# A three-stage kernel on one core: the last layer's products on the two row halves of TensorE

## The chip, the cores and the metric

The kernel runs on one core of one Trainium2 chip. The metric is the device time of one execution in microseconds (us), as the median of several runs. Engines are named as in the profile: PE is TensorE's matmul, PEld its weight load, DVE VectorE, ACT ScalarE, POOL GpSimd, SP the engine that issues most DMAs.

## What is computed

Causal attention for 2 batches of 12 heads, sequence 448, head size 64; its output, 896 rows of 768, goes through two blocks of two matrix products each:

```
attn_out = softmax(mask(q @ k.T / 8)) @ v            # (2, 12, 448, 64)
x = attn_out.transpose(0, 2, 1, 3).reshape(896, 768)
h = x @ w_in;  g = max(h, 0) + alpha * min(h, 0)      # 768 -> 2048, layer 1
x = g @ w_out                                         # 2048 -> 768, layer 2
h = x @ w_in2; g = h if h >= 1, 0 if h <= -1, else (h + 1)^2 / 4   # layer 3
out = g @ w_out2                                      # 2048 -> 768, layer 4
```

The weights of the two blocks are eight-byte floats; all else is f32.

## The kernel before, in words

Attention comes first and is pipelined over 12 head pairs; in it, `scores` (line 448) multiplies the two heads of a pair on the two row halves of TensorE, 64 rows each, into two banks of PSUM, and for the last tile of a head pair line 441 multiplies all 128 rows. Both are plain f32.

Then `run_layer` runs the four layers one after another. Activations lie transposed in SBUF: 128 rows of a feature tile by 448 tokens of a batch b (0 or 1), as a pair of planes in the type fp32r, the rounded value and the rest (`x_t`, `g_t`). A weight is split into two such parts by `Weights`: a chunk is loaded on SP (`load`, L109), its high words pass ACT (`magnitude`, L122), DVE rebuilds f32 values from integer halves in four steps (L141 to L160), ACT rounds (L169) and DVE takes the rest (L173). Three buffers hold split chunks, two the raw words.

Layers 2 and 4 have 6 output tiles m of 128 features, and for each 4 chunks of 4 feature tiles: 16 steps k. `products` issues for each k three products per batch: high weight with both planes, low weight with the high plane. Each is one matmul of 128 rows, 128 columns of weights and 448 moving columns, with its own weight load; that is 6 x 16 x 6 = 576 matmuls in layer 4. Layers 1 and 3 have as many with 16 tiles f of 6 steps.

PSUM has 8 banks here: three buffers of two banks (`pair`, pool ps_s) and two of one bank (`single`, pools ps_3 and ps_o). A tile m takes one pair, a bank for each batch; the last tile of layer 4 takes the two single banks, and its last chunk does all products of b = 0 before those of b = 1.

The order of instructions on each engine is the order of the code (`manual_schedule`). After the products of a chunk, `interleave` issues the split steps of a later chunk in turn with what is `late`: the moving out of the tile before. For layer 4 that is `evac_out`: ACT copies the first 224 columns and SP stores them, DVE copies the other 224 and ACT's queue stores them. The last tile has `evac_first` for b = 0 and `evac_last` for b = 1, which copies 320 and 128 columns on DVE.

Of the kernel before, what the change touches and what calls it, by code (L numbers as in the profile page):

```python
# [8 lines left out]
F32 = mybir.dt.float32  # L9
# [13 lines left out]
def attention_moe_moe_kernel(ctx: ExitStack, tc: tile.TileContext, qk, v, w1, w2, w3, w4, alpha, out):  # L23
# [8 lines left out]
    nc = tc.nc  # L32
    NP, _, _, S = qk.shape
    NB = 2
# [251 lines left out]

        return [high, low]

    def evac_out(ps, m, b):
        o = ep.tile([128, S], F32, tag="act_g", name="o_sb")  # L290

        def store():
            for i, (copy, queue) in enumerate(((nc.scalar.copy, nc.sync), (nc.vector.tensor_copy, nc.scalar))):
                c = slice(i * S // 2, (i + 1) * S // 2)
                copy(o[:, c], ps[:, c])  # L295
                queue.dma_start(out=out[m * 128:(m + 1) * 128, b * S + c.start:b * S + c.stop], in_=o[:, c])

        return [store]

    def evac_first(ps, m, b):  # L300
        for op in evac_out(ps, m, b):
            op()

    def evac_last(ps, m, b):
        o = ep.tile([128, S], F32, tag="act_g", name="o_sb")
        for c, queue in ((slice(0, 320), nc.sync), (slice(320, S), nc.scalar)):
            nc.vector.tensor_copy(o[:, c], ps[:, c])
            queue.dma_start(out=out[m * 128:(m + 1) * 128, b * S + c.start:b * S + c.stop], in_=o[:, c])

    def interleave(a, b):  # L310
        a, b = list(a), list(b)
        while a or b:
            for ops in (a, b):
                if ops:
                    ops.pop(0)()

    def pair():
        return ps_s.tile([128, 2, 512], F32, tag="s", name="ps")

    def single(pool):  # L320
        return pool.tile([128, 512], F32, tag="s", name="ps1")

    def products(ps, ws, src, k, kk, first, last):

        for part in range(2):
            for b in ps:
                for xp in range(2 - part):
                    nc.tensor.matmul(  # L328
                        ps[b][:, :S],
                        lhsT=ws[:, part, k * 128:(k + 1) * 128],  # L330
                        rhs=src[b, kk][:, xp],
                        start=first and part == 0 and xp == 0,
                        stop=last and part == 1,
                    )

    def early_tile():

        ws = wts.next()
        ps = {b: single((ps_3, ps_o)[b]) for b in range(NB)}
        early[0] = ws, ps  # L340
        for part in FILL:
            for b, ks in part:
                for k in ks:
                    products({b: ps[b]}, ws, x_t, k, k, k == 0, False)
            yield

    def run_layer(layer, late):

        if layer in (1, 3):
            mt, nch, kc, src = NF, 1, KD, x_t  # L350
        else:
            mt, nch, kc, src = NM, NC2, KC, g_t
        evac = {1: act_prelu, 2: evac_x, 3: act_quad, 4: evac_out}[layer]
        for m in range(mt):
            ps = {}
            for ch in range(nch):
                if layer == 1 and m in early:
                    ws, ps = early.pop(m)
                    products(ps, ws, src, kc - 1, kc - 1, False, True)
                else:  # L360
                    ws = wts.next()
                if ch == 0 and layer == 4 and m == mt - 1:
                    rest = {b: single((ps_3, ps_o)[b]) for b in range(NB)}
                elif ch == 0:
                    t = None if ps else pair()
                    rest = {} if ps else {b: t[:, b] for b in range(NB)}
                else:
                    rest = ps

                end = layer == 4 and m == mt - 1 and ch == nch - 1  # L370
                for group in [{b: p} for b, p in rest.items()] if end else [rest] if rest else []:
                    for k in range(kc):
                        kk = ch * kc + k
                        products(group, ws, src, k, kk, kk == 0, kk == nch * kc - 1)
                    if end:
                        for b, p in group.items():
                            (evac_last if b == NB - 1 else evac_first)(p, m, b)
                ps = {**ps, **rest}
                if wts.n_used > 1 and not early:
                    interleave(wts.split_ops(), late)  # L380
                    late = []
                    wts.run(wts.load())
                    wts.run(wts.magnitude())
            late = [] if end else [op for pair in zip(*(evac(ps[b], m, b) for b in range(NB))) for op in pair]
        return late


    class Attention:
# [143 lines left out]
        def evac(self, p):  # L532
            b, m = divmod(p, NP // NB)
            return evac_x(self.o.pop(p), m, b)

    with tc.manual_schedule():
# [4 lines left out]
        def step(gen, n):  # L541
# [4 lines left out]
        ps_s, ps_3, ps_o = (  # L546
            ctx.enter_context(tc.tile_pool(name=f"ps_{n}", bufs=b, space=PSUM))
            for n, b in (("s", 3), ("3", 1), ("o", 1))
        )
        with ExitStack() as pa:  # L550
# [12 lines left out]
            at.clear_v()  # L563
            early = {}
            fill = early_tile()
            steps = wts.prime()
            prime = []
# [96 lines left out]
        ep = ctx.enter_context(tc.tile_pool(name="ep", bufs=2))  # L664
        late = []
        for layer in (1, 2, 3, 4):
            late = run_layer(layer, late)
            if layer % 2 == 0:
                interleave(late, [])
                late = []  # L670
# [44 lines left out]
```

## Time and profile before

| | us |
|---|---|
| runs | 545.83, 547.82, 545.70 |
| median | 545.83 |
| span of the profiled execution | 544.2 |
| TensorE matmul busy in it | 538.2 |
| weight load, DVE, ACT, POOL busy | 476.0, 416.4, 240.9, 138.5 |
| layer 4, first to last matmul's start | 423.4 to 539.9 |

The span goes from the first to the last instruction of one profiled execution, whose time beside the span is not given; the median of the runs is 1.6 us above it. The groups of the page's part 5 count instructions of one line with their mean duration. A matmul's duration overlaps its neighbours', so the pace of a stream is the distance of starts.

### The profile page before, as it was taken

What the parts mean: (1) busy time and instruction counts of PE and PEld (TensorE: products, weight loads), DVE (VectorE), ACT (ScalarE), POOL (GpSimd) and SP (SyncE); (2) the same over time, 40 slices, a digit from 0 to 9 for tenths busy, and PEclk for the clock granted to TensorE, in tenths of its full rate; (3) what the DMA queues carried; (4) which work ended last, traced back from release to release, by engine and by line L of the source; (5) the groups of instructions that cost most, each with busy time, mean ns of one, the idle gap of its engine ahead of it and who ended that gap; (6) DMA issues with size and microseconds to landing.
All of it is one profiled execution on the core that took longest, in us unless ns stands there. A gap on an engine that the chain in (4) does not pass through costs nothing.

```text
span 544.2 us, 8503 instructions
## 1 busy us (share of the span) xinstructions
PE 538.2 (99%) x3055; PEld 476.0 (87%) x3055; DVE 416.4 (77%) x790; ACT 240.9 (44%) x504; POOL 138.5 (25%) x190
## 2 busy tenths in 40 slices
PE   8999999999999999999999999999999999999997
PEld 4666689999999999999999999999999999999996
DVE  5899879888889987576566699888898865755740
ACT  7999953333333333232323255555555332322310
POOL 5777822333333420000000023333333200000000
PEclk9999999999999999999999999999999999999999
DMA  6555313333332234342344333333322243434421
GB/s 186 185 157 171 91 59 117 116 117 116 117 93 80 88 91 134 97 142 92 94 139 120 114 119 113 117 116 117 115 70 70 95 144 123 151 111 133 136 71 34
DMA packets 25339, 61.90 MB, mean 114 GB/s; under 512 B 3537, under 2 KB 13009, under 8 KB 25297
## 3 DMA queue, kind: packets, MB, share of 16 engines
q1 hardware_dynamic: 22992, 59.58, 34.8%
q10 hardware_dynamic: 2304, 1.79, 1.0%
q8 instruction: 24, 0.39, 0.3%
q14 instruction: 19, 0.15, 0.1%
HBM read 58.60 MB, written 2.75 MB: 113 GB/s over the span
## 4 chain that ended last, share of the span: by engine, by line
PE 93%; ACT 3%; DVE 1%; POOL 1%; issue 0%; DVEq 0%; POOLq 0%
PE ps L328 86%; PE ps L527 3%; ACT pexp L468 2%; PE ps L448 2%; PE ps L510 1%; PE ps L441 1%; POOL pexp L485 1%; PE ps L71 1%; DVE pexp L459 1%; DVE pt L616 0%; ACT pt L634 0%; ACT pt L632 0%; ACT x L282 0%; ACT w_split L169 0%; ACT pt L633 0%
## 5 line engine op out<-in xcount | busy, mean ns | idle before, releaser
L328 PE MATMUL ps<-x,w_split 128*128 128x448 f32 x1152 | 234.2, 365 | 0.0
L328 PE MATMUL ps<-g,w_split 128*128 128x448 f32 x1152 | 233.8, 365 | 0.0
L328 PEld LDWEIGHTS ps<-g,w_split 128*128 128x128 f32 x1152 | 216.4, 188 | 17.1
L328 PEld LDWEIGHTS ps<-x,w_split 128*128 128x128 f32 x1152 | 216.2, 188 | 17.1
L246 POOL TENSOR_TENSOR g<-act_g,g 128x448 fp32r<-128x448 f32 x64 | 85.6, 1338 | 265.7 <-ACT g L245 265.6
L169 ACT CAST w_split<-w_f 128x512 fp32r<-128x512 f32 (+2 forms) x81 | 56.8, 701 | 126.8 <-DVE w_f L160 87.0
L173 DVE TENSOR_TENSOR w_split<-w_f,w_split 128x512 fp32r<-128x512 f32 (+1 forms) x78 | 64.1, 822 | 50.2 <-ACT w_split L169 50.0
L245 ACT CAST g<-act_g 128x448 fp32r<-128x448 f32 x64 | 36.2, 565 | 76.5 <-DVE act_g L258 66.5
L141 DVE TENSOR_SCALAR w_f<-w_f 128x512 f32<-128x512 f32 (+2 forms) x81 | 58.5, 722 | 8.3 <-ACT w_f L122 8.2
L154 DVE SCALAR_TENSOR_TENSOR w_f<-w_raw,w_f 128x512 uint32<-128x512 uint32 (+2 forms) x81 | 63.7, 786 | 1.5
L160 DVE SCALAR_TENSOR_TENSOR w_f<-w_raw,w_f 128x512 uint32<-128x512 uint32 (+2 forms) x81 | 63.6, 786 | 1.4
L122 ACT ACTIVATE w_f<-w_raw 128x512 f32<-128x512 f32 (+2 forms) x84 | 62.0, 739 | 0.1
L468 ACT ACTIVATE pexp<-pexp,stat 128x128 f32<-128x128 f32 (+3 forms) x84 | 43.7, 527 | 2.3 <-DVE stat L459 2.0
L485 POOL TENSOR_SCALAR pexp<-pexp,stat 128x384 f32<-128x384 f32 (+3 forms) x79 | 39.9, 527 | 15.0 <-DVE stat L477 13.8
L147 DVE TENSOR_SCALAR w_f<-w_f 128x512 uint32<-128x512 uint32 (+2 forms) x81 | 38.5, 475 | 1.5
L270 ACT ACTIVATE act_t<-act_t,half 128x448 f32<-128x448 f32 x32 | 21.5, 671 | 37.3 <-DVE act_t L269 37.3
L459 DVE CUSTOM_DVE_ANT_0 pexp<-ps,mask 128x128 f32<-128x128 f32 (+3 forms) x84 | 33.4, 447 | 5.0 <-POOL ident masks.py:199 3.5
L285 DVE TENSOR_TENSOR x<-ps,x 128x448 fp32r<-128x448 f32 x24 | 14.8, 618 | 17.5 <-ACT x L282 17.5
L295 DVE COPY o_sb<-ps 128x224 f32<-128x224 f32 x11 | 4.3, 392 | 28.3 <-ACT o_sb L295 28.3
L448 PEld LDWEIGHTS ps<-qk 64*128 64x128 f32 x144 | 12.9, 196 | 12.7 <-DVE pt L629 4.6
L527 PE MATMUL ps<-pt,v 128*64 128x448 f32 (+3 forms) x192 | 23.2, 385 | 0.0
L269 DVE TENSOR_SCALAR act_t<-ps 128x448 f32<-128x448 f32 x32 | 19.8, 620 | 2.8 <-PE ps L328 2.2
(45 smaller groups left out, 236.9 us busy)
## 6 DMA issues: line engine op xcount, KB each, us to landing
w_raw<-w SPq DMA_DIRECT2D x48, 512.0 KB, 3.6
w_raw<-w SPq DMA_DIRECT2D x29, 768.0 KB, 4.3
qk<-qk SPq DMA_DIRECT2D x10, 448.0 KB, 3.8
w_raw<-w SPq DMA_DIRECT2D x9, 256.0 KB, 4.2
out<-o_sb SPq DMA_DIRECT2D x11, 112.0 KB, 1.7
out<-o_sb ACTq DMA_DIRECT2D x11, 112.0 KB, 1.7
v<-v SPq DMA_DIRECT2D x12, 56.0 KB, 3.8
v<-v SPq DMA_DIRECT2D x12, 48.0 KB, 3.3
```

What stands on the lines that cost most here:

```text
L122: nc.scalar.activation(out=f32(w[:, c]), in_=f32(hi[:, c]), func=AF.Abs)
L141: nc.vector.tensor_scalar(out=f32(w[:, c]), in0=f32(w[:, c]), scalar1=HI_MIN, scalar2=HI_MAX, op0=ALU.max, op1=ALU.min)
L154: nc.vector.scalar_tensor_tensor(out=w[:, c], in0=hi[:, c], scalar=0xC0000000, in1=w[:, c], op0=ALU.bitwise_and, op1=ALU.bitwise_or)
L160: nc.vector.scalar_tensor_tensor(out=w[:, c], in0=lo[:, c], scalar=29, in1=w[:, c], op0=ALU.logical_shift_right, op1=ALU.bitwise_or,)
L169: nc.scalar.copy(s[:, 0, c], f32(w[:, c]))
L173: (side or nc.vector).tensor_sub(s[:, 1, c], f32(w[:, c]), f32(s[:, 0, c]))
L246: nc.gpsimd.tensor_sub(t[:, 1, :], g, f32(t[:, 0, :]))
L328: nc.tensor.matmul(ps[b][:, :S], lhsT=ws[:, part, k * 128:(k + 1) * 128], rhs=src[b, kk][:, xp], start=first and part == 0 and xp == 0, st ...
L459: nc.vector.tensor_tensor_reduce(out=self.pexp[p][:, o:o + w], in0=b[:, :w], in1=mask3 if i == 3 else mask[:, 384 - w:], scale=-SCALE, sca ...
L468: nc.scalar.activation(out=e, in_=e, func=AF.Exp, bias=self.st[p][:, 0, n:n + 1], scale=-1.0, accum_out=self.st[p][:, 1, n:n + 1],)
L485: nc.gpsimd.tensor_scalar(out=e, in0=e, scalar1=self.st[p][:, 2, n:n + 1], scalar2=1.0, op0=ALU.mult, op1=ALU.mult)
L527: nc.tensor.matmul(ps[j * D:(j + 1) * D, c * 128:S], lhsT=t[:, c, j, :], rhs=pt[:, 2 * c + j, c * 128:], start=c == 0, stop=c == NQ - 1,)
```

## The change

In layer 4 each product becomes two, on rows 0 to 63 and on rows 64 to 127, each half into a bank of its own; ACT copies the second half's bank to SBUF and DVE adds the first half's bank to it when the tile is moved out. A tile m takes four banks: two pairs for even m, one pair and the two single banks for odd m.

```
-    def evac_out(ps, m, b):
+    def evac_out(ps, m, b, parts=((0, S),)):
         o = ep.tile([128, S], F32, tag="act_g", name="o_sb")
+        t = ep.tile([128, S], F32, tag="act_t", name="o_half")
 
         def store():
-            for i, (copy, queue) in enumerate(((nc.scalar.copy, nc.sync), (nc.vector.tensor_copy, nc.scalar))):
-                c = slice(i * S // 2, (i + 1) * S // 2)
-                copy(o[:, c], ps[:, c])
-                queue.dma_start(out=out[m * 128:(m + 1) * 128, b * S + c.start:b * S + c.stop], in_=o[:, c])
+            for i, (lo, hi) in enumerate(parts):
+                c = slice(lo, hi)
+                nc.scalar.copy(t[:, c], ps[1][:, c])
+                nc.vector.tensor_add(o[:, c], ps[0][:, c], t[:, c])
+                queue = nc.scalar if (i + b) % 2 else nc.sync
+                queue.dma_start(out=out[m * 128:(m + 1) * 128, b * S + lo:b * S + hi], in_=o[:, c])
...
     def evac_last(ps, m, b):
-        o = ep.tile([128, S], F32, tag="act_g", name="o_sb")
-        for c, queue in ((slice(0, 320), nc.sync), (slice(320, S), nc.scalar)):
-            nc.vector.tensor_copy(o[:, c], ps[:, c])
-            queue.dma_start(out=out[m * 128:(m + 1) * 128, b * S + c.start:b * S + c.stop], in_=o[:, c])
+        for op in evac_out(ps, m, b, ((0, 256), (256, S))):
+            op()
...
+    def products_rows(ps, ws, src, k, kk, first, last):
+
+        for part in range(2):
+            for b in ps:
+                for xp in range(2 - part):
+                    for h in range(2):
+                        r = slice(h * 64, h * 64 + 64)
+                        nc.tensor.matmul(
+                            ps[b][h][:, :S],
+                            lhsT=ws[r, part, k * 128:(k + 1) * 128],
+                            rhs=src[b, kk][r, xp],
+                            start=first and part == 0 and xp == 0,
+                            stop=last and part == 1,
+                        )
+
+    def four_banks(m):
+
+        t = [pair(), pair()] if m % 2 == 0 else [pair()]
+        banks = [t_[:, i] for t_ in t for i in range(2)]
+        if m % 2:
+            banks += [single(ps_3), single(ps_o)]
+        return {b: banks[2 * b:2 * b + 2] for b in range(NB)}
...
-                if ch == 0 and layer == 4 and m == mt - 1:
-                    rest = {b: single((ps_3, ps_o)[b]) for b in range(NB)}
+                if ch == 0 and layer == 4:
+                    rest = four_banks(m)
...
-                        products(group, ws, src, k, kk, kk == 0, kk == nch * kc - 1)
+                        (products_rows if layer == 4 else products)(
+                            group, ws, src, k, kk, kk == 0, kk == nch * kc - 1
+                        )
```

On PE, the end of the last chunk (g1_12 to g1_15 are feature tiles of b = 1; a row counts matmuls in a row with the same bank and the same tile) reads before:

```order
L328 MATMUL ps1_5024<-g0_15_4299,w_split_5091 128x448 x3
L328 MATMUL ps1_5025<-g1_12_4125,w_split_5091 128x448 x3
L328 MATMUL ps1_5025<-g1_13_4189,w_split_5091 128x448 x3
L328 MATMUL ps1_5025<-g1_14_4253,w_split_5091 128x448 x3
L328 MATMUL ps1_5025<-g1_15_4305,w_split_5091 128x448 x3
```

and with the change, for the last of these rows:

```order
L344 MATMUL ps1_5514<-g1_15_4330,w_split_5627 128x448
L344 MATMUL ps1_5515<-g1_15_4330,w_split_5627 128x448
L344 MATMUL ps1_5514<-g1_15_4330,w_split_5627 128x448
L344 MATMUL ps1_5515<-g1_15_4330,w_split_5627 128x448
L344 MATMUL ps1_5514<-g1_15_4330,w_split_5627 128x448
L344 MATMUL ps1_5515<-g1_15_4330,w_split_5627 128x448
```

The three matmuls of a step into one bank have become six, in turn into two.

On ACT, from the last weight chunk to the end of the kernel (ps1 are single banks, o_half is the copy of the second half), before:

```order
L122 ACTIVATE w_f32_5065<-w_raw_5018 128x512
L169 CAST w_split_5091<-w_f32_5065 128x512
L295 COPY o_sb_5134<-ps1_5024 128x224
L296 DMA out<-o_sb_5134 128x224
L308 DMA out<-o_sb_5151 128x128
```

and with the change:

```order
L169 CAST w_split_5627<-w_f32_5577 128x512
L296 COPY o_half_5707<-ps_5513 128x448
L296 COPY o_half_5736<-ps1_5515 128x256
L299 DMA out<-o_sb_5735 128x256
L296 COPY o_half_5736<-ps1_5515 128x192
```

ACT has two copies of the last tile where it had none, and the DMA issue of that tile's first part now stands between them.

On DVE, where a tile m is moved out between the split steps of a weight chunk, before:

```order
L141 TENSOR_SCALAR w_f32_4869<-w_f32_4869 128x512
L295 COPY o_sb_4871<-ps_4722 128x224
L147 TENSOR_SCALAR w_f32_4869<-w_f32_4869 128x512
L295 COPY o_sb_4872<-ps_4722 128x224
L154 SCALAR_TENSOR_TENSOR w_f32_4869<-w_raw_4832,w_f32_4869 128x512
```

and with the change:

```order
L141 TENSOR_SCALAR w_f32_5259<-w_f32_5259 128x512
L297 TENSOR_TENSOR o_sb_5261<-ps_5016,o_half_5262 128x448
L147 TENSOR_SCALAR w_f32_5259<-w_f32_5259 128x512
L297 TENSOR_TENSOR o_sb_5263<-ps1_5017,o_half_5264 128x448
L154 SCALAR_TENSOR_TENSOR w_f32_5259<-w_raw_5198,w_f32_5259 128x512
```

The two copies of 224 columns have become two adds of 448, at the same places.

## Rows read from the trace of the kernel before

**Rows 1.** Page, parts 1 and 2: busy us (share), and granted clock in tenths.

```profile
PE 538.2 (99%) x3055; PEld 476.0 (87%) x3055; DVE 416.4 (77%) x790; ACT 240.9 (44%) x504; POOL 138.5 (25%) x190
...
PEclk9999999999999999999999999999999999999999
```

**Rows 2.** Chain of waits from 423.4 us to the end: start, length, what.

```profile
423.34 116.95 PE ps L328 x577
540.29 0.02 issue
540.32 0.49 DVE o_sb L307
540.81 0.20 DVEq L711
```

**Rows 3.** Source view of L328 from 330 us: ns min/median/max, first and last start.

```profile
L328 PEld LDWEIGHTS ps<-g,w_split x576: 187/188/188, 423.2 to 539.7; 128*128 128x128 f32 x192
L328 PE MATMUL ps<-g,w_split x576: 362/365/369, 423.4 to 539.9; 128*128 128x448 f32 x192
```

**Rows 4.** Windows of layer 4: length, busy us of each engine, clock, DMA.

```profile
423.00:443.00 20.00, 20.00 (x100) 18.54 (x99) 14.62 (x24) 7.14 (x12) 2.71 (x2) 1.00 0.32 105
443.00:462.00 19.00, 19.00 (x95) 17.61 (x95) 11.96 (x22) 5.47 (x10) 0.00 (x0) 1.00 0.43 136
...
521.00:541.00 20.00, 19.28 (x96) 17.52 (x94) 7.02 (x14) 2.71 (x6) 0.00 (x0) 1.00 0.11 35
```

**Rows 5.** Timeline, narrow windows near 7 us (start, length, engine, line): f32, all rows.

```profile
7.04 0.54 PE L441 MATMUL ps<-qk,qd 128*128 128x448 f32 x1
7.41 0.54 PE L441 MATMUL ps<-qk,qd 128*128 128x448 f32 x1
7.79 0.54 PE L441 MATMUL ps<-qk,qd 128*128 128x448 f32 x1
```

**Rows 6.** Timeline, narrow windows at 41 us: all rows, then pairs of row halves.

```profile
40.66 0.54 PE L441 MATMUL ps<-qk,qd 128*128 128x448 f32 x1
41.13 0.59 PE L448 MATMUL ps<-qk 64*128 64x384 f32 x2
...
41.56 0.49 PE L448 MATMUL ps<-qk 64*128 64x384 f32 x2
41.88 0.38 PE L448 MATMUL ps<-qk 64*128 64x256 f32 x2
41.88 0.19 PEld L448 LDWEIGHTS ps<-qk 64*128 64x128 f32 x2
42.09 0.38 PE L448 MATMUL ps<-qk 64*128 64x256 f32 x2
42.10 0.19 PEld L448 LDWEIGHTS ps<-qk 64*128 64x128 f32 x2
```

**Rows 7.** Waits from 423 us (total us, times, longest); then groups (busy us, mean ns).

```profile
ACT w_split L169 <- PE ps L328: 10.6, 4, 2.7
...
L328 PE MATMUL ps<-g,w_split 128*128 128x448 f32 x576 | 116.9, 365 | 0.0
L328 PEld LDWEIGHTS ps<-g,w_split 128*128 128x128 f32 x576 | 108.2, 188 | 8.5
```

**Rows 8.** Timeline of DVE at 419 us: the end of f = 14 in layer 3.

```profile
419.42 0.62 DVE L273 TENSOR_TENSOR act_g<-ps,act_t 128x448 f32<-128x448 f32 x1
```

**Rows 9.** Groups by line and shape, 78 us to the end: busy us, mean ns, idle.

```profile
L282 ACT CAST x<-ps 128x448 fp32r<-128x448 f32 x12 | 5.8, 536 | 18.0 <-PE ps L328 18.0
L295 ACT COPY o_sb<-ps 128x224 f32<-128x224 f32 x11 | 3.8, 347 | 31.1 <-PE ps L328 26.7 <-DVE w_f L147 4.4
...
L285 DVE TENSOR_TENSOR x<-ps,x 128x448 fp32r<-128x448 f32 x13 | 8.0, 621 | 16.6 <-ACT x L282 16.6
L295 DVE COPY o_sb<-ps 128x224 f32<-128x224 f32 x11 | 4.3, 392 | 28.3 <-ACT o_sb L295 28.3
L307 DVE COPY o_sb<-ps 128x320 f32<-128x320 f32 x1 | 0.5, 492 | 1.6 <-PE ps L328 1.6
L307 DVE COPY o_sb<-ps 128x128 f32<-128x128 f32 x1 | 0.3, 281 | 0.0
```

**Rows 10.** Timeline of the end: start us, length, engine, line, [idle before].

```profile
537.92 0.35 ACT L295 COPY o_sb<-ps 128x224 f32<-128x224 f32 x1 [9.40 <-PE ps L328]
538.30 0.33 SPq L296 DMA_DIRECT2D out<-o_sb  x1
538.30 0.39 DVE L295 COPY o_sb<-ps 128x224 f32<-128x224 f32 x1 [9.05 <-ACT o_sb L295]
...
539.91 0.37 PE L328 MATMUL ps<-g,w_split 128*128 128x448 f32 x1
540.32 0.69 DVE L307 COPY o_sb<-ps 128x320 f32<-128x320 f32 x2 [1.62 <-PE ps L328]
540.84 0.33 SPq L308 DMA_DIRECT2D out<-o_sb  x1
541.04 0.34 ACTq L308 DMA_DIRECT2D out<-o_sb  x1
```

## The prediction

> **What bounds the kernel now.** I read the profile's first two parts: in [rows 1] the reader sees TensorE busy for 538.2 of 544.2 us, weight loads 476.0, VectorE 416.4, and a granted clock in the top tenth in every slice. Then the chain of waits from 423.4 us on, where the last layer begins [rows 2]: one piece of products, 116.95 us, then only 0.7 us of VectorE and queue. Nothing outside TensorE's matmul stream ends anything in this stage. The source view of L328 [rows 3] gives its pace: 576 matmuls on g, first start 423.4, last 539.9, so 116.5 / 575 = 0.2026 us from start to start. The windows of the stage [rows 4] give a granted clock of 1.00 throughout, which is the 2.4 GHz level. At that level 448 columns, one each cycle, are 448 / 2.4 = 186.7 ns. So each matmul takes **16 ns more** than its columns, and 576 × 16 = 9.2 us of the layer are this excess. What the change can win is inside those 9.2 us; all else it does is on engines with room or at the very end.
>
> **What the trace says of row halves.** Attention has them already: line 448 multiplies 64 rows at a time, each half into its own bank, in plain f32. Compare it with line 441, plain f32 over all 128 rows. In [rows 5] three neighbouring starts of 448-column matmuls are 7.04, 7.41 and 7.79: 0.375 us each, two cycles per column (0.3733) and about 2 ns. In [rows 6] two half matmuls start together (the rows count x2) at 41.56, the next two at 41.88, the next two at 42.09 us: 0.32 us for a pair of 384 columns (two cycles each: 0.320) and 0.21 to 0.22 for a pair of 256 (0.2133). So a **pair of halves takes the time of one full matmul**, not of two and not less. Their two weight loads are together as well: 0.19 us for two, as long as one of all rows lasts (188 ns, [rows 3]). That supports replacing one full product by two half products at no cost, and it shows no gain, because per row half the columns to stream and the columns to load stay the same: 448 and 128.
>
> **The change part by part.**
>
> *Products.* Out go 576 full matmuls, in come 1152 half matmuls, 576 pairs, each with the columns of the one it replaces. The clock stays at its level, since the stream has no gaps. Where is the 16 ns from? The full f32 row shows about 2 ns of it in any matmul; the other 14 belong to this one-cycle-per-column form with a load beneath each, which no row shows in halves. Bounds from rows: the pair runs like the f32 rows, 0.1867 + 0.002 = 0.1887, a gain of 0.0139 × 576 = 8.0 us; or the 14 ns are paid by each half's load in turn, 0.2026 + 0.0139, a loss of 8.0 us. The far end is two halves in turn, 2 × 0.2026. I take **0.2026, change 0.0**: the nearest rows are the full form in this stage and the pairs of line 448, where halving rows changed nothing in time per column. An excess that came from a load reading beside a stream would come in both halves at once, since both load at once.
>
> The Trainium skill, page "TensorE: Matmul & The Clock Gate", section "The mechanism", says a weight load overlaps a matmul in flight only when the row group differs; that speaks for the change. Here 188 ns loads lie under matmuls of the same rows, 108.2 us of loads in 116.9 ([rows 7]), so this trace does not bear it out beyond the 14 ns; by that rule the sum would be the first rival's. The Trainium skill, page "TensorEngine Tiling (Array Packing)", section "Theoretical Speedup", speaks against it: it gives a gain only where a dimension is at most 64, and this contraction has 128; the sum by it would be the one I take.
>
> *Change of mode.* From full rows to halves in attention: 40.66 to 41.13 is 0.47 us where 0.375 is the pace [rows 6], so 0.1 us, once, where layer 4 begins. **+0.1 us.**
>
> *Banks.* An m tile takes four banks instead of two. At the start of the layer the second pair is the one of f = 14 in layer 3, whose last reader ends at 419.42 + 0.62 = 420.04 us [rows 8], 3.3 us before the first product at 423.4. After that even and odd m use different banks, so a bank is reused after a whole tile of about 19.4 us, and its readers need about 2.5. **0.**
>
> *Moving a tile out.* Per (m, b) a 224-column copy on each of ACT and VectorE (347 and 392 ns) becomes a 448-column copy on ACT (like line 282, 536 ns) and an add of 448 on VectorE (like line 285, 621 ns) [rows 9]. Per m tile that is 2 × 229 = 0.46 us more on VectorE and 0.38 on ACT. VectorE is busy 11.96 of 19 us in such a stretch [rows 4]. The low_bits and high_bits steps of the weight chunk stand behind the adds on VectorE, and the hi_part cast behind the store's DMA issue on ACT; who waits for those is a chunk whose cast already waits for TensorE to free its buffer (10.6 us in 4 waits, [rows 7]), so the chunks are ahead. On SP the store of b = 0 now waits for the add, about 0.8 us later, and the next weight load behind it waits for a raw buffer that VectorE frees later still. The cover is that lead; if it were gone, 0.46 us for each of 5 tiles, 2.3 us, would show. **0.**
>
> *The end.* Before: the last matmul starts at 539.91, VectorE copies 320 and 128 columns from 540.32, and the last DMA is issued at 541.04 [rows 10], 0.72 us after the first copy began. Now for b = 1 the order on ACT is copy 256, DMA issue (which waits for the add of 256), copy 192; the add of 192 and its SP issue follow. ACT copies: 347 ns at 224 and 536 at 448 give 0.37 for 256 and 0.32 for 192. Adds: 621 at 448, less 1.1 ns a column (from 0.492 at 320 and 0.281 at 128), 0.41 and 0.34. Issue on ACT 0.34, four hand-overs of about 0.03 (538.27 to 538.30), 0.05 for the sequencer. In all 0.37 + 0.41 + 0.34 + 0.05 + 0.32 + 0.34 + 0.12 = 1.95 against 0.72: **+1.2 us**. If ACT can start its second copy without the issue's 0.34, it is 0.9. The tile of b = 0 is stored under b = 1's last 12 products (2.4 us).
>
> **Sum:** 0 + 0.1 + 0 + 0 + 1.2 = +1.3 us on the profiled span of 544.2, so 545.5. The runs shown have a median of 545.83, 1.6 us above that span; I leave that rest as it is: **547.1 us**, +0.24%. A measurement of this kernel can tell about 0.5% from no change, 2.7 us.
>
> **The rivals.**
>
> *The load's share goes away.* If the 14 ns are the price of a full-array load under a full-array matmul, and a half's load hides under the other half, a pair takes 0.1887: -8.0 + 1.3 = -6.7, **539.1 us**. For it: full f32 matmuls have 2 ns of excess and these 16, so something in the one-cycle form is not hidden. Against it: the halves run in step, so a half's load lies beside its own half's matmul as before. It passes the 0.5% line once 7 ns a pair are won (4.0 us).
>
> *Two loads, two excesses* (the other side). The 14 ns are a stall that each load gives the whole array, and a pair has two loads: 0.2165 a pair, +8.0 + 1.3, **555.1 us**. Place: the weight loads of L344, every pair. It decides from 2.5 ns a pair ((2.7 - 1.3) / 576). For it: the loads double from 576 to 1152. Against it: in line 448 two loads at once cost no more than one.
>
> *No overlap.* The halves of this form take turns, and the change doesn't do what it says: 576 × 0.2026 = +116.7 us, **664 us**. For it: line 448's pairs write each bank at half the pace that these would. Against it: those pairs are in step in every row read.
>
> *The lead is used up* on VectorE or the tail is longer than summed: +2.3 more, **549.4 us**.
>
> **How the numbers follow.** The forecast 0.52 (its own range 546.0 to 548.5), the load's share 0.20, two excesses 0.15, no overlap 0.06, lead used up 0.07. The range runs from the first rival's time to the second's, 539.0 to 555.5, and leaves out turns and what lies beyond. Faster by over 0.5%: 0.20. Within: the forecast and a third of the last, 0.54. Slower: 0.15 + 0.06 + the rest of the last, 0.26.
>
> **What would show it.** In the profile after: 576 pairs of g matmuls from about 423.4, starts of pairs 0.203 apart (0.189: first rival; 0.216: second; 0.405: turns), weight loads x1152, the chain still one piece of products, VectorE waiting for TensorE and not the reverse, and between the last matmul and the last DMA issue 2.3 us instead of 1.1. A wait of TensorE on VectorE or ACT anywhere after 423 us, or a granted clock under 1.00, would make the sum wrong.

## The result and the profile after

The changed kernel takes **548.86 us** (median of 5 runs, 548.55 to 549.68) against 545.70 us; the ratio is 1.0051, 95% interval 1.0033 to 1.0069. It is half a percent slower: the forecast's sign and range held, its size did not (+1.3 us were summed; the ratio gives 2.8, the medians differ by 3.2).

The profiled execution has a span of 547.0 us, 2.8 more than before. The page's parts 1 and 2, first lines:

```profile
span 547.0 us, 9642 instructions
PE 539.7 (99%) x3631; PEld 475.8 (87%) x3631; DVE 418.7 (77%) x790; ACT 243.2 (44%) x506; POOL 138.2 (25%) x190
...
PEclk9999999999999999999999999999999999999999
```

The counts of TensorE grew by 576, VectorE and ScalarE are busy 2.3 us longer each, and the clock stayed where it was in [rows 1]. The chain of waits from the start of layer 4 (start, length, what) answers to [rows 2]:

```profile
423.05 119.24 PE ps L344 x1146
...
542.38 0.38 ACT o_half L296
...
542.78 0.44 DVE o_sb L297
...
543.24 0.34 ACTq L299
...
543.62 0.33 ACT o_half L296
...
543.97 0.36 DVE o_sb L297
```

Still one piece of products, and no wait of TensorE on another engine; the products are 119.24 us instead of 116.95, and behind them stands a chain of five steps. The source view of L344 (ns min/median/max, first and last start) gives the pace, as [rows 3] did:

```profile
L344 PEld LDWEIGHTS ps<-g,w_split x1152: 182/184/186, 423.0 to 541.7; 64*128 64x128 f32 x192
L344 PE MATMUL ps<-g,w_split x1152: 358/365/469, 423.0 to 541.9; 64*128 64x448 f32 x192
```

576 pairs from 423.0 to 541.9: 118.9 / 575 = 0.2068 us a pair, against 0.2026 for a full matmul. The end, to be read beside [rows 10]:

```profile
541.28 1.00 PE L344 MATMUL ps<-g,w_split 64*128 64x448 f32 x6
...
542.38 0.37 ACT L296 COPY o_half<-ps 128x256 f32<-128x256 f32 x1 [1.95 <-PE ps L344]
542.78 0.42 DVE L297 TENSOR_TENSOR o_sb<-ps,o_half 128x256 f32<-128x256 f32 x1 [1.69 <-ACT o_half L296]
543.24 0.34 ACTq L299 DMA_DIRECT2D out<-o_sb  x1
543.62 0.32 ACT L296 COPY o_half<-ps 128x192 f32<-128x192 f32 x1 [0.87 <-DVE o_sb L297]
543.97 0.36 DVE L297 TENSOR_TENSOR o_sb<-ps,o_half 128x192 f32<-128x192 f32 x1 [0.76 <-ACT o_half L296]
544.35 0.33 SPq L299 DMA_DIRECT2D out<-o_sb  x1
```

From the last matmul's start (541.9) to the last DMA issue are 2.44 us, before 1.13; from that issue to the end of the span 2.65, before 3.16. So the 2.8 us of the two spans are: layer 4 began 0.4 earlier (423.0 for 423.4; attention and layers 1 to 3 are unchanged, so this is a difference between two executions), its products took 118.9 - 116.5 = **2.4 us longer**, the way from the last matmul to the end **0.8 us longer**.

### The profile page after: what moved, and what is told of

Its sections match the earlier page's. It is cut to its first block, busy times and chain, and to the rows that moved or that the text cites. A ratio compares the mean times of both kernels' runs of the same rounds, so it can differ in the third digit from the quotient of the medians.

```text
span 547.0 us, 9642 instructions
## 1 busy us (share of the span) xinstructions
PE 539.7 (99%) x3631; PEld 475.8 (87%) x3631; DVE 418.7 (77%) x790; ACT 243.2 (44%) x506; POOL 138.2 (25%) x190
## 4 chain that ended last, share of the span: by engine, by line
PE 92%; ACT 4%; DVE 2%; POOL 1%; DMA 1%; ACTq 0%; issue 0%; POOLq 0%
PE ps L329 64%; PE ps L344 22%; PE ps L553 3%; ACT pexp L494 2%; PE ps L474 2%; PE ps L536 1%; PE ps L467 1%; DMA qk<-qk 1%; POOL pexp L511 1%; DVE pexp L485 1%; DVE pt L642 0%; ACT pt L660 0%; ACT pt L658 0%; ACT x L282 0%; ACTq L445 0%
## 5 line engine op out<-in xcount | busy, mean ns | idle before, releaser
L344 PE MATMUL ps<-g,w_split 64*128 64x448 f32 x1152 | 119.3, 364 | 0.0
L344 PEld LDWEIGHTS ps<-g,w_split 64*128 64x128 f32 x1152 | 108.6, 184 | 10.6 <-issue 0.3
L329 PE MATMUL ps<-g,w_split 128*128 128x448 f32 x576 | 116.9, 365 | 0.0
L329 PEld LDWEIGHTS ps<-g,w_split 128*128 128x128 f32 x576 | 108.2, 188 | 8.6
L297 DVE TENSOR_TENSOR o_sb<-ps,o_half 128x448 f32<-128x448 f32 (+2 forms) x13 | 7.6, 586 | 29.8 <-ACT o_half L296 29.8
L285 DVE TENSOR_TENSOR x<-ps,x 128x448 fp32r<-128x448 f32 x24 | 14.8, 619 | 15.7 <-ACT x L282 15.7
```

Of the source, the lines that this page charges most:

```text
L329: nc.tensor.matmul(ps[b][:, :S], lhsT=ws[:, part, k * 128:(k + 1) * 128], rhs=src[b, kk][:, xp], start=first and part == 0 and xp == 0, st ...
L344: nc.tensor.matmul(ps[b][h][:, :S], lhsT=ws[r, part, k * 128:(k + 1) * 128], rhs=src[b, kk][r, xp], start=first and part == 0 and xp == 0, ...
```

## The experiments

All traces are read for the distance of starts in layer 4; the granted clock there is 1.00 in every one. "From single starts" means the start times of single matmuls in the trace, which are finer than the views' tenths. Each short diff is against the changed kernel, unless it says otherwise. Runs without a time are one execution each, and the time of a kernel that leaves work out is not compared.

**The halves undone, all else kept.** All 128 rows again, spread over the two banks by plane; the rest is the change's:

```
-                    for h in range(2):
-                        r = slice(h * 64, h * 64 + 64)
...
+                    h = xp if part == 0 else 0
...
+                        ps[b][h][:, :S],
+                        lhsT=ws[:, part, k * 128:(k + 1) * 128],
+                        rhs=src[b, kk][:, xp],
```

> Layer 4 with matmuls of all 128 rows again, spread over the change's two banks by plane; copy, add, order of banks and tail as in the change. If the row halves cost the 4.0 ns a pair that the trace of the change shows (206.7 against 202.7 ns from start to start), the pace goes back to 202.7 ns and the layer's 576 products to 116.5 us from first to last start, and what is left over the kernel before is the tail alone: 0.8 to 1.3 us, some 546.5 to 547.0 us. If the copies, adds and bank order slow TensorE, the pace stays near 206.7 and the time near 548.9.

Measured: 546.52 us (11 runs) against 545.58, ratio 1.0023, interval 1.0014 to 1.0032. The source view:

```profile
L343 PE MATMUL ps<-g,w_split x576: 361/366/370, 422.9 to 539.4; 128*128 128x448 f32 x192
```

116.5 / 575 = 0.2026 again. Copies, adds and banks cost TensorE nothing; the tail costs 0.0023 × 545.6 = 1.3 us (0.8 to 1.7 by the interval). The rest of the change's loss is the pace of the halves: in the traces the products are 2.4 us longer with them and no longer with all rows.

**One half alone.** Products on rows 0 to 63 only, into two banks by plane (`r = slice(0, 64)`), so the other half of every contraction is left out.

> Products on rows 0 to 63 only, 576 instead of 1152; rows 64 to 127 of every contraction are left out. Theory 1, the two halves compete: one half alone runs at 202.7 ns from start to start. Theory 2, a 64-row matmul is slower in itself: 206.7 ns. Either way the layer's end moves by no more than 2.4 us.

```profile
L344 PE MATMUL ps<-g,w_split x576: 359/365/465, 425.0 to 543.9; 64*128 64x448 f32 x192
```

118.9 / 575 = 0.2068 us: a half alone is as slow as the pair. (Its layer began at 425.0, 2 us late, with the code before it unchanged: so much can two executions differ there.) The halves don't compete; the theory of two stalls, one for each load, falls here, and so does the one of a load hidden under the other half.

**384 columns.** `[:, :384]` on the moving side, the output and the moving out, in the form with all rows and in the change.

> As the kernel with all 128 rows and two banks by plane, but with 384 moving columns in layer 4; the last 64 tokens of each batch are left out. Columns alone take 160.0 ns. If the 16 ns excess of a full matmul belongs to each matmul or its load, the pace is 176.0 ns; if it grows with the columns, 160.0 x 202.7 / 186.7 = 173.7 ns.

> The change with 384 moving columns in layer 4; the last 64 tokens of each batch are left out. If the 20 ns excess of a pair of halves belongs to the pair or its loads, the pace of pairs is 180.0 ns; if it grows with the columns, 160.0 x 206.7 / 186.7 = 177.1 ns. If the excess of the full form grows and the 4 ns do not, 177.7 ns.

The source view of the first and of the second:

```profile
L344 PE MATMUL ps<-g,w_split x576: 334/334/338, 423.9 to 523.5; 128*128 128x384 f32 x192
```

```profile
L345 PE MATMUL ps<-g,w_split x1152: 328/331/442, 422.9 to 522.7; 64*128 64x384 f32 x192
```

99.6 / 575 = 0.1732 us for a full matmul and 99.8 / 575 = 0.1736 for a pair; between single starts the trace has 173.3 ns in both, 13.3 above the 160.0 of the columns. At 384 columns **the halves cost nothing**. "64 rows are slower" falls as well. None of the written numbers for the halves was right; for all rows 173.7 was near.

**Six widths in one run.** Each tile m of layer 4 with another number of moving columns, taken across the two planes where over 448 (`w = W4[m]`, `W4 = (512, 464, 456, 440, 432, 416)`).

> All 128 rows, two banks by plane, and another number of moving columns in each of the six tiles m of layer 4: 512, 464, 456, 440, 432, 416. Tokens are left out or taken from the neighbouring plane. Theory 1, a flat excess of 32 array cycles as at 384 columns, and an irregular 38 at 448 from a step in which starts are granted: 226.7, 206.7, 203.3, 196.7, 193.3, 186.7 ns, some of them up to 6.7 more. Theory 2, the excess grows with the columns from 13.3 ns at 384 to 16.0 at 448: 232, 210, 206, 199, 196, 190 ns.

> The change with 512, 464, 456, 440, 432, 416 moving columns in the six tiles m; tokens are left out or taken from the neighbouring plane. Theory 1, starts are granted in steps of 16 array cycles (6.7 ns; 26 steps at 384 columns, 31 at 448): pairs at multiples of 6.7 ns, 226.7 or 233.3, 206.7 or 213.3, 206.7 or 213.3, 200.0, 193.3 or 200.0, 186.7 or 193.3. Theory 2, the 4 ns are a fixed price of a 64-row matmul above some width: the pace of the full form at the same width plus 0 or 4 ns.

Source views of windows inside three of the tiles, all rows and then halves:

```profile
L345 PE MATMUL ps<-g,w_split x88: 389/389/389, 424.8 to 444.5; 128*128 128x512 f32 x88
L345 PE MATMUL ps<-g,w_split x90: 367/372/376, 445.8 to 464.5; 128*128 128x464 f32 x90
...
L345 PE MATMUL ps<-g,w_split x85: 344/352/354, 524.2 to 540.0; 128*128 128x416 f32 x85
```

```profile
L346 PE MATMUL ps<-g,w_split x176: 386/386/394, 424.7 to 444.5; 64*128 64x512 f32 x176
L346 PE MATMUL ps<-g,w_split x180: 364/369/373, 445.8 to 464.5; 64*128 64x464 f32 x180
...
L346 PE MATMUL ps<-g,w_split x170: 341/348/351, 524.2 to 540.0; 64*128 64x416 f32 x170
```

Row by row the same pace: 19.7 / 87 and 19.8 / 87, 18.7 / 89 twice, 15.8 / 84 twice. From single starts, the settled pace in ns, the same for both forms within 0.3:

| columns | 384 | 416 | 432 | 440 | 448 | 456 | 464 | 512 |
|---|---|---|---|---|---|---|---|---|
| pace | 173.3 | 188.1 | 195.6 | 200.8 | 202.7 or 206.7 | 206.6 | 210.0 | 226.7 |
| over columns / 2.4 GHz | 13.3 | 14.8 | 15.6 | 17.5 | 16.0 or 20.0 | 16.6 | 16.7 | 13.3 |

The excess doesn't grow with the columns (232 was written for 512) and it isn't flat: it is least at 384 and 512. The flat theory's allowance of up to 6.7 ns more covers all six paces, so it wasn't tested sharply. For halves, multiples of 6.7 ns fall (210.0, 200.8, 195.6, 188.1 are none), and so does a price of 64 rows above some width: only at 448 did the two forms differ.

**Weights of 64 columns.** `lhsT=ws[..., k * 128:k * 128 + 64]`, half the output features left out, in both forms.

> All 128 rows, two banks by plane, 448 moving columns, but weights of 64 columns; features 64 to 127 of every output tile are left out. If the excess of 16 ns is the price of the load beneath a matmul, half of its 13.3 goes: 196 ns. If it belongs to the matmul's form, 202.7 ns stay.

> The change with weights of 64 columns; features 64 to 127 of every output tile are left out. If the load sets the excess, pairs come at 196 to 200 ns; if the 64-row form does, at 206.7 ns as before.

The group by shape and the source view of the form with all rows, then the source view with halves:

```profile
L343 PEld LDWEIGHTS ps<-g,w_split 128*64 128x64 f32 x571 | 76.3, 134 | 39.1
```

```profile
L343 PE MATMUL ps<-g,w_split x576: 360/362/369, 423.2 to 539.5; 128*64 128x448 f32 x192
```

```profile
L344 PEld LDWEIGHTS ps<-g,w_split x1152: 129/130/133, 423.1 to 539.3; 64*64 64x64 f32 x192
L344 PE MATMUL ps<-g,w_split x1152: 357/359/416, 423.1 to 539.5; 64*64 64x448 f32 x192
```

With all rows a load fell from 188 to 134 ns and the pace stayed: 116.3 / 575 = 0.2023 us. **The excess is not the price of the load.** That excludes both of the prediction's middle rivals at their root. Pairs did not stay: their loads fell from 184 to 130 ns and their pace from 0.2068 to 0.2024, which neither written number has (196 to 200, or 206.7). So the 4 ns of the halves went away with the shorter load, and the excess of 16 ns did not; why, this run alone doesn't tell.

**Two paces at 448 columns?** A few throw-away matmuls ahead of tiles m = 1 to 5, in the change and in the form with all rows. Without them pairs keep 0.2068 us and full matmuls 0.2026 from the first tile to the last:

```
+    KICK = ((), (512,) * 4, (64,) * 4, (384,) * 4, (256,), (440,))
...
+        for w in KICK[m]:
+            for h in range(2):
+                r = slice(h * 64, h * 64 + 64)
+                nc.tensor.matmul(
+                    ps[0][h][:, :w], lhsT=ws[r, 0, :128], rhs=src[0, 0].rearrange("p a s -> p (a s)")[r, :w],
+                    start=True, stop=True,
+                )
```

> The change with a few throw-away pairs of matmuls ahead of tiles m = 1 to 5 of layer 4: four of 512 columns, four of 64, four of 384, one of 256, one of 440. Theory 1, 448 columns have two paces, 202.7 and 206.7 ns, and what ran just before sets which one a row half falls into: after some of these the pairs come at 202.7 ns in step, after others at 206.7. Theory 2, 206.7 ns is the only pace of 64 rows at 448 columns: after every one of them the pairs come at 206.7 ns. The throw-away pairs take about 2.4 us in all.

> The same throw-away matmuls ahead of the same tiles, but all 128 rows with two banks by plane. Theory 1: after at least one of them the full matmuls run at 206.7 ns too. Theory 2: 202.7 ns after every one.

Source views of a window inside each tile, m = 0 to 5; the change with throw-away pairs:

```profile
L345 PE MATMUL ps<-g,w_split x177: 364/365/366, 424.6 to 442.8; 64*128 64x448 f32 x177
L345 PE MATMUL ps<-g,w_split x181: 358/362/367, 444.8 to 463.0; 64*128 64x448 f32 x181
L345 PE MATMUL ps<-g,w_split x172: 358/362/367, 465.7 to 482.9; 64*128 64x448 f32 x172
L345 PE MATMUL ps<-g,w_split x183: 364/365/366, 484.6 to 503.5; 64*128 64x448 f32 x183
L345 PE MATMUL ps<-g,w_split x182: 364/365/366, 504.8 to 523.4; 64*128 64x448 f32 x182
L345 PE MATMUL ps<-g,w_split x150: 358/362/367, 524.8 to 539.8; 64*128 64x448 f32 x150
```

and all 128 rows:

```profile
L344 PE MATMUL ps<-g,w_split x88: 362/365/369, 424.7 to 442.3; 128*128 128x448 f32 x88
L344 PE MATMUL ps<-g,w_split x91: 362/365/369, 444.6 to 462.9; 128*128 128x448 f32 x91
L344 PE MATMUL ps<-g,w_split x83: 362/365/369, 465.8 to 482.4; 128*128 128x448 f32 x83
L344 PE MATMUL ps<-g,w_split x89: 368/368/368, 484.7 to 502.9; 128*128 128x448 f32 x89
L344 PE MATMUL ps<-g,w_split x89: 368/368/368, 504.7 to 522.9; 128*128 128x448 f32 x89
L344 PE MATMUL ps<-g,w_split x76: 362/365/369, 524.7 to 539.9; 128*128 128x448 f32 x76
```

The reader can tell the paces by the spread of durations: even (364 to 366, 368 throughout) in one, uneven (358 to 367, 362 to 369) in the other. Full rows at m = 2: 16.6 / 82 = 0.2024; at m = 3: 18.2 / 88 = 0.2068. From single starts: 202.7 ns after 512, 64 and 440 columns, 206.7 after 384 and 256, **in halves and full rows alike**, for the rest of the tile; only m = 0 differs, 206.7 in halves and 202.7 in full rows. In the halves 512 turned the slow pace into the fast one, in both forms 384 turned the fast one into the slow and 440 turned it back; 64 and 256 left it as it was. Theory 1 holds: 448 columns have two paces, either is kept for a whole tile, what ran just before can change it, and each form runs at both. Each throw-away width was tried at one place only in either form, so whether its width or something else about it turns the pace isn't shown.

**A cut that avoids 448.** The kernel before with its 896 tokens cut at 512 and 384 in layers 1 to 4 (against the kernel before, cut short):

```
+    CUTS = ((0, 512), (512, 2 * S))
...
-                        ps[b][:, :S],
+                        ps[b][:, :b[1] - b[0]],
...
-                        rhs=src[b, kk][:, xp],
+                        rhs=src[kk][:, xp, b[0]:b[1]],
```

> The kernel before with the 896 tokens of layers 1 to 4 cut at 512 instead of at 448 (tile 0 of layer 1 keeps its two halves). From the paces at 512 and 384 columns, a pair of products takes 226.7 + 173.3 = 400.0 ns in place of 2 x 202.7 = 405.3. If the flat 13.3 ns at these widths holds in all layers and the other engines keep up, 1134 pairs save 6.0 us: 539.6 us. If VectorE becomes the bound in layers 1 and 3, where it is busy 86% of the time, only layers 2 and 4 save, 3.1 us: 542.5 us. If the excess comes back in some other way: 545.6 us.

Measured: 554.73 us, ratio 1.0169 (1.0154 to 1.0185), a miss. The timeline around 440 us, narrow windows (each row is the first of the matmuls then in flight):

```profile
439.96 0.63 PE L339 MATMUL ps<-g,w_split 128*128 128x512 f32 x2
440.20 0.57 PE L339 MATMUL ps<-g,w_split 128*128 128x512 f32 x2
440.43 0.75 PE L339 MATMUL ps<-g,w_split 128*128 128x384 f32 x3
440.61 0.57 PE L339 MATMUL ps<-g,w_split 128*128 128x384 f32 x2
440.79 0.57 PE L339 MATMUL ps<-g,w_split 128*128 128x512 f32 x2
```

Starts 0.24, 0.23, 0.18, 0.18 apart: 0.83 us for two of each width in place of 0.80. Where the width changes after one or two matmuls (four times in the six of a step) the low pace is never reached: from single starts a matmul takes 206.7 ns on average from layer 1 to layer 4, and 4.0 ns more for 2268 matmuls are 9.1 us, where 8.9 were measured. So the width was kept for a whole chunk:

```
-                for group in [{b: p} for b, p in rest.items()] if end else [rest] if rest else []:
+                for group in [{b: rest[b]} for b in sorted(rest, reverse=not end and (m if nch == 1 else ch) % 2 == 1)]:
```

> As with the tokens cut at 512, but in each weight chunk all products of one cut come before those of the other, and every second chunk in the opposite order, so that the width changes once a chunk (80 chunks) and not four times a step. If the flat 13.3 ns hold wherever the width stays the same for 12 matmuls or more, 1134 pairs save 5.3 ns each, 6.0 us, less 20 ns for each change of width, 1.6 us: 541.2 us. If what a matmul pays depends on more than its neighbour's width, so that the 235 and 178 ns of the run with alternating widths stay, it is at 554.7 us again.

Measured: **542.29 us** (542.21 to 543.14) against 545.80, ratio 0.9937, interval 0.9923 to 0.9951. It beats both kernels. The source view of layer 4:

```profile
L339 PE MATMUL ps<-g,w_split x576: 333/367/398, 421.4 to 537.2; 128*128 128x512 f32 x96, 128*128 128x384 f32 x96
```

115.8 us from first to last start, where the kernel before has 116.5. Of the 4.4 us written (6.0 less 1.6 for the changes of width) some 3.5 came. After each change of width it takes six to nine matmuls to settle: from single starts over the four layers, 512 columns average 228.1 ns and 384 average 174.3, not 226.7 and 173.3.

## Why the prediction was right, and where its sum was off

- **Products, summed as 0.0: the mis-sized term.** They cost +2.4 us, 0.2068 against 0.2026 us a pair. The step that failed is "I take 0.2026": it assumed that the full form in that stage has one pace. It has two at 448 columns, and the change's stream ran in the slower. The 4 ns a pair even pass the 2.5 from which the second rival was to decide, but that rival's mechanism isn't what ran. That the time stayed in the range is owed to the range's width (539.0 to 555.5), and the sign would have held by the tail alone. The halves themselves are free, as argued: in step at 384, 512 and all other widths, and at 202.7 ns at 448 after the right throw-away pairs.
- **That the halves run at once** was right: 1152 matmuls took 118.9 us; in turns they would have taken 233. No overlap is out.
- **The load's share goes away, and two loads, two excesses:** both put the 14 ns on the load. With half the columns to load the pace of the full form moved by 0.4 ns, that of pairs by 4.4, and never by 14; and one half alone, with one load, has the pair's pace. Both are out as mechanisms. The Trainium skill, page "TensorE: Matmul & The Clock Gate", section "The mechanism", would have a load overlap only matmuls of other rows; here the 188 ns load lay under a matmul of its own rows in every run with all 128 rows and full weights, and a load of 134 ns in its place moved the pace by 0.4 ns.
- **Change of mode, +0.1:** layer 4's first half pair starts 0.29 us after the last full matmul's (422.69 to 422.98 in the trace), 0.09 over the pace. But the second pair starts 0.31 us after the first, another 0.1 over, and [rows 6] had this too: 41.13 to 41.56 is 0.43 us for a pair of 0.32. So about 0.2 us, half of it inside the 2.4 of the products.
- **Banks and moving out, 0:** right. No wait of TensorE after 423 us, and with the halves undone the pace was the old one. The weight chunks stayed ahead: ACT's cast still waited 12.2 us in 4 waits for TensorE to free a buffer (10.6 in [rows 7]).
- **The end, +1.2:** to the last DMA issue it is 2.44 - 1.13 = 1.31, each step as summed (copies 0.37 and 0.32, adds 0.42 and 0.36, issue 0.34). To the end of the span only 0.8, because 2.65 us follow the last issue instead of 3.16; the run with the halves undone puts the whole tail at 0.8 to 1.7 us. Sized about right.
- **The chances:** the forecast's 546.0 to 548.5 was passed by 0.4 us; the measured +0.5% lies on the line that was drawn between no change and slower.

Not settled: why 448 columns have two paces, and why the switch from full rows to halves leaves the stream in the slow one. The switch alone doesn't do it: with weights of 64 columns the same switch left the pairs at 0.2024 us.

## What to carry to other kernels

A stream of matmuls that never waits still has a pace of its own; take it from the distance of starts, ask which term of a change could move it by a few ns, and multiply by the count. Here 4 ns × 576 were most of the loss. The pace depended on the moving width and on what ran before; 64 rows or 128 made no difference by themselves, and the length of the weight load made one only for halves at 448 columns. Before building a new form, run the old one at two or three widths: cutting 896 columns as 512 and 384, with the width kept for a chunk, gave 0.6% where splitting rows lost 0.5%.

## What the runs showed of the hardware

- With fp32r operands at a granted clock of 1.00, the time above one column a cycle is 13.3 ns at 384 and 512 columns and up to 17.5 at the widths tried between; at 448 it is 16.0 or 20.0 by history.
- A matmul of 64 rows takes as long as one of 128 (0.2068 against 0.2026 or 0.2068 at 448, the same elsewhere), and two on the two halves take no longer than one.
- The halves need not be in step: early in the changed kernel's layer 4 one half ran at 202.7 and the other at 206.7 ns, falling 4 ns further behind with each pair for some 107 pairs, until the fast one was two matmuls ahead (427 ns). From there both ran at 206.7, and at the end the last three starts (541.50, 541.71, 541.91) are the slow half's alone. So the slow half set the pace throughout; the matmuls that signal a finished chunk, each the chunk's last and so on rows 64 to 127, mark the fast one. In the run with throw-away pairs, the same code in tile m = 0 ran both halves at 206.7 from the start, so this is not the same in every execution.
- Where 512 and 384 columns alternate after one or two matmuls, they cost 233 to 238 ns at 512 and 176 to 180 at 384.
